# Storing both split parts of a weight tile and reading them back by GpSimd transfers, in an attention and two-expert-layer kernel

## The chip, the core and the metric

The kernel runs on one core of a Trainium2 chip. The metric is the device time of one execution in microseconds (us), the median over several runs. A profile is the record of one execution; its rows name the engines PE (TensorE matmul), PEld (TensorE weight load), DVE (VectorE), ACT (ScalarE), POOL (GpSimd) and SP (SyncE, which here only issues transfers).

## What is computed

Attention over 4 batches, 12 heads, 448 tokens and head size 64 with normed queries and keys, then two feed-forward layers on the 1792 tokens of 768 features:

```python
q_n, k_n = rmsnorm(q, g_q), rmsnorm(k, g_k)
attn = softmax(q_n @ k_n.T / sqrt(64))
x = attn @ v                                  # (4*448, 768)
h = x @ w_in                                  # 768 -> 2048
x = where(h > 0, h, exp(min(h, 0)) - 1) @ w_out          # 2048 -> 768
xn = x / rms(x) * rms_g
x = (silu(xn @ w_gate) * (xn @ w_val)) @ w_out2          # 768 -> 1536 -> 768
```

Everything is float32 in DRAM, and the result is wanted to about that precision.

## The kernel before

**Products.** A float32 product is made of three products of split operands: each operand is cut into a high part, rounded to the type that TensorE multiplies at one pass (F32R), and a low part, the rest (`split_w`, `split_x`, `split_g`). `mm3` multiplies high by high, high by low and low by high into one bank of PSUM. Data lie transposed, features on partitions, 448 tokens of one batch in a row; one matmul is 128x128 by 128x448.

**Stages.** `STAGES` has five. Stage 0 is the first layer for batch 0, stage 1 the same for batch 1, stage 2 the second layer for batches 0 and 1, stage 3 the first layer for batches 2 and 3, stage 4 the second layer for batches 2 and 3. The attention of batch 0 fills the first 75 us or so; that of the later batches is woven into stages 0 to 2. Where two batches stand together (from the second group of stage 2 on, `PLAIN`), four blocks of weights and four of data are multiplied as a "quad" of seven block products instead of eight (`quad`, `take_duo`), which wants sums and differences of weight blocks.

**Weights.** `wst` is a stream of chunks of 6 blocks of 128x128, 64 bits a weight. `w_convert` loads a raw chunk (768 KB, ring `wr` of two tiles), and ACT or POOL and DVE make it a float32 chunk (ring `wc`, three tiles). `w_f32` stores that chunk to DRAM (`kept`, 384 KB) at its first use, and later uses load it from there. `split_w` then makes the split tile (ring `w`, four tiles of two parts, 768 KB each; from stage 3 on two more, shown as `late`): a copy that rounds (ACT, DVE or POOL), and a subtraction (DVE or POOL). For a quad, `w_split` first makes sums and differences of two chunks in `p` tiles (four subtractions of half chunks), then splits four tiles, of which the fourth is half as wide. So each use of a weight costs a load, a copy and a subtraction, and that of a quad's weights the sums besides. `w_ahead` keeps as many tiles split ahead of the matmuls as the ring has.

**Between the stages.** Before a second layer, `norm` sums squares on TensorE, takes a root on ACT and a reciprocal on DVE (448 columns, one for each batch). The data of the next stage's quads are combined and split too (`combo`).

**Order.** All instructions are collected as operations with prices (`plan.add`). `Plan.schedule` lays them out by a list scheduler with a random seed and a number of passes, picks the engine where an operation has several (`alts`), and issues them in that order. Each engine then works its list in order. All transfers but a few small ones stand in SP's list, so a transfer whose data aren't ready holds back those behind it. Line numbers in the profile are those of a helper (L331, L334 in the changed kernel); operations are told apart by tiles.

Of the kernel before, what the change touches and what calls it, by code (L numbers as in the profile page):

```python
# [10 lines left out]
F32 = mybir.dt.float32  # L11
# [9 lines left out]
P = 128  # L21
# [15 lines left out]
class Plan:  # L37
# [4 lines left out]
    PASSES = 22  # L42
    SEED = 17
# [131 lines left out]
    def forward(self, rank):  # L175
# [35 lines left out]
        while left:  # L211
# [95 lines left out]
def kernel(ctx: ExitStack, tc: tile.TileContext, dims, tok, qk, vr, gq, gk, wst, rmsg, ident_in, out):  # L307
# [114 lines left out]
    def transposes(pairs):  # L422
        def go():
            for o, i in pairs:
                T.transpose(o, i, ident)

        plan.add({"pe": (0.02 + 0.11 * len(pairs), go)}, [o for o, _ in pairs], [i for _, i in pairs] + [ident], lag=0.16)
# [159 lines left out]
    def steps_of(kind, plain):  # L587
        nums = list(one if kind == 1 else two)
        res, k = [], 0
        nf = NF1 if kind == 1 else 2 * NF2  # L590
        for g in range(len(nums) // (nf + OG)):
            if g < plain:
                res += [("c", n) for n in nums[k:k + nf + OG]]
                k += nf + OG
# [8 lines left out]
            k += nf + OG  # L603
        return res

    stream = [st for s, (kind, _) in enumerate(STAGES) for st in steps_of(kind, PLAIN[s])]
# [7 lines left out]
    uses = {}  # L614
    for kind, _ in STAGES:
        for n in one if kind == 1 else two:
            uses[n] = uses.get(n, 0) + 1

    def w_f32(n):
# [5 lines left out]
        if uses[n] > 1:  # L625
# [13 lines left out]
    def w_split():  # L639
# [7 lines left out]
        if j == 0:  # L647
# [6 lines left out]
            duo["c"] = (c0, sa, sb, c1[:, HW:WN])  # L654
        spl_w[i] = split_w(duo["c"][j], HW if j == 3 else WN)

# [167 lines left out]
    def s_group(i, *gs):  # L824
# [17 lines left out]
        block(mms, (0.0 if gs == (0,) else 0.3) + 0.62 * len(gs))  # L842
# [82 lines left out]
    def pv(i, kts):  # L925
# [13 lines left out]
        block(mms, 0.14 + 0.866 * len(kts))  # L939
# [82 lines left out]
    def mm3(o, w, x, first, last):  # L1022
        wh, wl = w
        xh, xl = x
        block([(o, wh, xh, first, False), (o, wh, xl, False, False), (o, wl, xh, False, last)], 0.612)
# [282 lines left out]
    def second_experts(bs, plain):  # L1308
# [6 lines left out]
        for f0 in range(0, CF2, NF2):  # L1315
            last = f0 + NF2 >= CF2
# [12 lines left out]
            yield from acc_units(bs, f0, NF2, f0 == 0, last, ob, True, o_done)  # L1329
# [37 lines left out]
    for s, (kind, bs) in enumerate(STAGES):  # L1367
# [9 lines left out]
        for step in first_experts(bs, s >= 3) if kind == 1 else second_experts(bs, PLAIN[s]):  # L1377
# [105 lines left out]
```

## Time and profile before

| | us |
|---|---|
| median of 3 runs | 1238.09 (1236.55 to 1240.48) |
| the profiled execution | 1236.46 |
| its span | 1234.7 |
| TensorE busy, of the span | 1201.6 (97%) |
| DVE, POOL, ACT busy | 883.5, 903.7, 720.9 |
| moved by DMA | 178.95 MB, 145 GB/s in the mean |

TensorE is the busiest engine by far, and 33.1 us of the span are left in which it does not multiply. The weights are at work in these stretches: stage 0 from about 95 to 277 us, stage 1 to 435, stage 2 to 735, stage 3 to 980, stage 4 to the end. POOL spends the largest share of its time on weights: 226.8 us on 120 subtractions `w<-wc,w`, 64.5 on 32 of `w<-p,w` and 45.4 on 48 copies `w<-wc`; ACT spends 77.8 us on 99 such copies. A busy share says little by itself here: the question in each stretch is whether TensorE waits, and for whom.

### The profile page before, as it was taken

What the parts mean: (1) busy time and instruction counts of PE and PEld (TensorE: products, weight loads), DVE (VectorE), ACT (ScalarE), POOL (GpSimd) and SP (SyncE); (2) the same over time, 40 slices, a digit from 0 to 9 for tenths busy, and PEclk for the clock granted to TensorE, in tenths of its full rate; (3) what the DMA queues carried; (4) which work ended last, traced back from release to release, by engine and by line L of the source; (5) the groups of instructions that cost most, each with busy time, mean ns of one, the idle gap of its engine ahead of it and who ended that gap; (6) DMA issues with size and microseconds to landing.
All of it is one profiled execution on the core that took longest, in us unless ns stands there. A gap on an engine that the chain in (4) does not pass through costs nothing.

```text
span 1234.7 us, 17825 instructions
## 1 busy us (share of the span) xinstructions
PE 1201.6 (97%) x6228; PEld 1009.7 (82%) x6228; DVE 883.5 (72%) x1332; ACT 720.9 (58%) x1413; POOL 903.7 (73%) x651
## 2 busy tenths in 40 slices
PE   3999999999999999999999999999999989999998
PEld 2557877778777787777999999999999979999998
DVE  6887988878544578645797899825435899397592
ACT  5996879768665678655564563643425843342240
POOL 3467888789655586746998899967566998698590
PEclk9999999999999999999999999999999999999999
DMA  7578788775444366644336545212112112112112
GB/s 258 183 234 257 264 291 271 259 229 162 152 138 128 125 202 229 197 140 159 128 129 222 177 168 191 77 53 77 53 52 64 40 51 65 51 65 77 40 52 90
DMA packets 65664, 178.95 MB, mean 145 GB/s; under 512 B 11039, under 2 KB 23333, under 8 KB 65573
## 3 DMA queue, kind: packets, MB, share of 16 engines
q1 hardware_dynamic: 56932, 168.82, 41.0%
q10 hardware_dynamic: 8640, 8.99, 2.5%
q8 instruction: 49, 0.80, 0.3%
q14 instruction: 43, 0.34, 0.1%
HBM read 139.86 MB, written 37.92 MB: 144 GB/s over the span
## 4 chain that ended last, share of the span: by engine, by line
PE 88%; DVE 5%; ACT 2%; DMA 2%; issue 1%; POOL 1%; SPq 0%; ACTq 0%; DVEq 0%
PE bank L331 88%; DVE tbig L331 2%; DMA wr<-wst 1%; DVE rw L331 1%; ACT tbig L331 1%; DVE w L331 1%; DMA ybig<-tok 0%; DMA rb<-scr 0%; ACT p L331 0%; DVE bank L331 0%; POOL w L331 0%; DVE ybig L331 0%; DVE ss L331 0%; DVE ql L331 0%; DMA wc<-kept 0%
## 5 line engine op out<-in xcount | busy, mean ns | idle before, releaser
L331 PE MATMUL bank<-gbig,w 128*128 128x448 f32 x1872 | 402.7, 369 | 1.4 <-DVE tbig L331 1.0
L331 PEld LDWEIGHTS bank<-gbig,w 128*128 128x128 f32 x1872 | 346.4, 188 | 37.6 <-issue 7.1
L331 PE MATMUL bank<-xs,w 128*128 128x448 f32 x1584 | 364.5, 371 | 1.8 <-DVE tbig L331 1.1
L331 PEld LDWEIGHTS bank<-xs,w 128*128 128x128 f32 x1584 | 290.6, 188 | 31.9 <-issue 7.1
L331 POOL TENSOR_TENSOR w<-wc,w 128x768 fp32r<-128x768 f32 (+1 forms) x120 | 226.8, 1892 | 54.4 <-ACT w L331 48.2
L331 DVE TENSOR_REDUCE bank<-bank 128x1 f32<-128x448 f32 x168 | 98.9, 624 | 42.8 <-PE bank L331 42.5
L331 ACT ACTIVATE w<-wc 128x768 fp32r<-128x768 f32 (+1 forms) x99 | 77.8, 786 | 74.0 <-PE bank L331 60.5
L331 ACT ACTIVATE p<-bank,nm,rr 128x448 f32<-128x448 f32 x126 | 90.3, 720 | 22.6 <-DVE nm L331 16.3
L331 DVE SCALAR_TENSOR_TENSOR wc<-wc,wt 128x768 int32<-128x768 int32 x68 | 88.3, 1298 | 21.0 <-ACT wc L331 12.4
L331 PE MATMUL bank<-late,w 128*128 128x448 f32 x420 | 100.6, 366 | 0.8 <-DVE w L331 0.8
L331 ACT ACTIVATE pt<-bank 128x384 f32<-128x384 f32 (+2 forms) x175 | 75.7, 451 | 22.9 <-PE bank L331 20.6
L331 POOL TENSOR_TENSOR gbig<-tbig,gbig 128x448 fp32r<-128x448 f32 x57 | 76.9, 1354 | 13.5 <-ACT gbig L331 12.8
L331 PEld LDWEIGHTS bank<-late,w 128*128 128x128 f32 x420 | 78.8, 188 | 7.7 <-DVE w L331 1.2
L331 POOL TENSOR_TENSOR w<-p,w 128x768 fp32r<-128x768 f32 x32 | 64.5, 2017 | 20.2 <-ACT w L331 19.7
L331 POOL TENSOR_SCALAR w<-wc 128x768 fp32r<-128x768 f32 (+1 forms) x48 | 45.4, 947 | 44.4 <-PE bank L331 35.1
L331 DVE TENSOR_TENSOR ybig<-bank,ybig 128x448 f32<-128x448 f32 x72 | 44.3, 620 | 44.2 <-PE bank L331 43.7
L331 PE MATMUL bank<-ident,p 128*128 128x128 f32 x441 | 70.8, 279 | 1.2 <-ACT pe L331 0.8
L331 ACT ACTIVATE wt<-wr 128x768 uint16<-128x768 uint8 x51 | 55.7, 1093 | 24.8 <-DVE wc L331 20.1
L331 PEld LDWEIGHTS bank<-ident,p 128*128 128x128 f32 x441 | 53.7, 142 | 19.0 <-ACT pt L331 3.3
L331 PE MATMUL bank<-xs,late 128*128 128x448 f32 x288 | 68.2, 366 | 0.9 <-DVE xs L331 0.6
L331 DVE TENSOR_SCALAR wt<-wr 128x768 uint16<-128x768 uint16 x68 | 68.5, 1008 | 0.3
L331 ACT ACTIVATE tbig<-bank 128x448 f32<-128x448 f32 x78 | 42.1, 541 | 39.8 <-PE bank L331 31.9
(237 smaller groups left out, 2229.2 us busy)
## 6 DMA issues: line engine op xcount, KB each, us to landing
wr<-wst SPq DMA_DIRECT2D x68, 768.0 KB
wc<-kept SPq DMA_DIRECT2D x100, 384.0 KB
kept<-wc SPq DMA_DIRECT2D x68, 384.0 KB
rw<-qk SPq DMA_DIRECT2D x21, 512.0 KB
tk<-tok SPq DMA_DIRECT2D x20, 480.0 KB
rv<-vr SPq DMA_DIRECT2D x24, 256.0 KB
out_t<-ybig SPq DMA_DIRECT2D x24, 224.0 KB
rb<-scr ACTq DMA_DIRECT2D x36, 128.0 KB
```

Source lines behind the costliest of these rows:

```text
L331: return lambda *a, **k: f(*[real(x) for x in a], **{n: real(x) for n, x in k.items()})
```

## The change

`store_parts` writes a split tile, both parts, to DRAM at its first use (768 KB, the half-wide tile 2 x 192 KB), unless the tile isn't used again. `load_parts` brings it back at each later use, by a transfer that GpSimd issues, so that copy, subtraction and sums fall away there. The float32 chunk is kept only where it is used both plainly and in a quad. Stage 4 takes its three groups of weights in the order 1, 2, 0 (`TURN`), where groups 1 and 2 were quads in stage 2 already, and group 0, which was plain there, still has its sums to be made. The scheduler gets other prices for a few TensorE blocks, 14 passes instead of 22 and seed 3 instead of 17, and so lays out everything anew.

In instructions of the program, before and after: `kept` stores 68 and 24, `kept` loads 100 and 24, stores of parts 0 and 92 (76 of 768 KB, 16 of 192 KB), GpSimd loads 0 and 136 (96 of 768 KB, 40 of 192 KB); on POOL, weight subtractions 176 and 89, weight copies 56 and 28, sums of `p` 86 and 54; on ACT, weight copies 167 and 80; on DVE, weight subtractions 48 and 19. The matmuls are the same in number and shape.

```diff
-    PASSES = 22
-    SEED = 17
+    PASSES = 14
+    SEED = 3
...
             if self.ops[i][4]:
-                if e == "sp":
+                if e == "g":
+                    dma_free = max(free[e], dma_free) + self.ops[i][2]
+                    done[i] = dma_free + self.DMA_LAT
+                elif e == "sp":
...
-        q, cost = (SP, 0.43) if by == "sp" else (A, 0.5)
+        q, cost = {"sp": (SP, 0.43), "a": (A, 0.5), "g": (G, 1.0)}[by]
...
+    TURN = {4: (1, 2, 0)}
...
+    def load_parts(k):
+        w = r_w.next()
+        if k[1] == 3:
+            for h in range(2):
+                dma(w[:, h, 0:HW], parts[k][:, h * HW:(h + 1) * HW], P * HW * 4, by="g")
+        else:
+            dma(w.rearrange("p a n -> p (a n)"), parts[k], P * WN * 8, by="g")
+        return w
...
+        parts[k] = tc.dram_tile([P, 2 * WN], F32, name=f"parts{len(parts)}")
+        dma(parts[k], w.rearrange("p a n -> p (a n)").bitcast(F32), P * WN * 8)
...
         c = w_convert(n)
-        if uses[n] > 1:
+        if n in plain_uses and n in in_quads:
...
         if st[0] == "c":
+            k = (st[1], 0)
+            if k in parts:
+                spl_w[i] = load_parts(k)
+                return
             spl_w[i] = split_w(w_f32(st[1]), WN)
+            if plain_uses[st[1]] > 1 or st[1] in in_quads:
+                store_parts(k, spl_w[i])
             return
...
+        if k in parts:
+            spl_w[i] = load_parts(k)
+            return
...
         spl_w[i] = split_w(duo["c"][j], HW if j == 3 else WN)
+        if quad_uses[n0, n1] > 1:
+            store_parts(k, spl_w[i])
...
-        for f0 in range(0, CF2, NF2):
-            last = f0 + NF2 >= CF2
+        for f0 in [NF2 * g for g in turn]:
+            last = f0 == NF2 * turn[-1]
```

The first rows of SP's list, before: `tok` and `qk` are inputs of the attention, `tk`, `wr`, `ybig` and `rw` tiles that hold them (the raw weight tiles `wr` serve for this at the start).

```order
L331 DMA tk_101<-tok 128x960
L331 DMA rsb_127<-gq 1x128
L331 DMA wr_91<-tok 128x960
L331 DMA rw_102<-qk 128x1024
L331 DMA rsb_127<-gk 1x128
L331 DMA ident<-ident_in 128x128
L331 DMA ybig<-tok 128x960
L331 DMA wr_92<-qk 128x1024
L331 DMA ybig<-tok 128x960
```

After:

```order
L334 DMA tk_101<-tok 128x960
L334 DMA wr_91<-tok 128x960
L334 DMA rsb_127<-gk 1x128
L334 DMA rsb_127<-gq 1x128
L334 DMA ident<-ident_in 128x128
L334 DMA ybig<-tok 128x960
L334 DMA rw_102<-qk 128x1024
L334 DMA wr_92<-qk 128x1024
L334 DMA ybig<-tok 128x960
```

The first load into `ybig` (`tok`, 480 KB) has moved ahead of the first load of `rw` (`qk`, 512 KB).

SP's list in the middle of stage 0, before: a raw weight load (`wr<-wst`, 768 KB) alternates with the store of a float32 chunk (`kept<-wc`, 384 KB).

```order
L331 DMA wr_92<-wst 128x1536
L331 DMA kept_157<-wc_94 128x768
L331 DMA wr_91<-wst 128x1536
L331 DMA tk_101<-tok 128x960
L331 DMA kept_158<-wc_95 128x768
L331 DMA wr_92<-wst 128x1536
L331 DMA kept_159<-wc_93 128x768
L331 DMA wr_91<-wst 128x1536
L331 DMA tk_101<-tok 128x960
L331 DMA kept_162<-wc_94 128x768
L331 DMA rw_102<-qk 128x1024
```

After:

```order
L334 DMA wr_91<-wst 128x1536
L334 DMA parts_155<-w_97 128x1536
L334 DMA parts_157<-w_98 128x1536
L334 DMA wr_92<-wst 128x1536
L334 DMA rw_102<-qk 128x1024
L334 DMA parts_159<-w_99 128x1536
L334 DMA wr_91<-wst 128x1536
L334 DMA tk_101<-tok 128x960
L334 DMA kept_162<-wc_95 128x768
L334 DMA parts_161<-w_100 128x1536
L334 DMA wr_92<-wst 128x1536
L334 DMA parts_163<-w_97 128x1536
```

The stores in between are now `parts<-w` of 768 KB, which wait for a finished split tile, and a raw load stands behind one or two of them.

DVE's list at the change from stage 3 to stage 4, before, up to the first of the two reciprocals of `norm`: three instructions make weight tiles of the next quads (`w_100<-p`, `w_99<-wc`, `p_107<-wc,wc`).

```order
L331 TENSOR_TENSOR bank_131<-bank_131,rsb_126 128x448
L331 TENSOR_TENSOR w_100<-p_106,w_100 128x768
L331 TENSOR_TENSOR tbig<-bank_130,rsb_126 128x448
L331 TENSOR_TENSOR gbig<-tbig,gbig 128x448
L331 TENSOR_TENSOR tbig<-bank_133,tbig 128x448
L331 TENSOR_TENSOR w_99<-wc_95,w_99 128x768
L331 TENSOR_TENSOR tbig<-tbig,ybig 128x448
L331 TENSOR_TENSOR xs_73<-ybig,xs_72 128x448
L331 TENSOR_TENSOR p_107<-wc_95,wc_93 128x384
L331 TENSOR_TENSOR tbig<-bank_132,tbig 128x448
L331 RECIPROCAL tbig<-tbig 128x448
```

After:

```order
L334 TENSOR_TENSOR tbig<-bank_130,rsb_126 128x448
L334 TENSOR_TENSOR xs_67<-ybig,xs_66 128x448
L334 TENSOR_TENSOR gbig<-tbig,gbig 128x448
L334 TENSOR_TENSOR tbig<-bank_133,tbig 128x448
L334 TENSOR_TENSOR late_5489<-ybig,late_5464 128x448
L334 TENSOR_TENSOR tbig<-bank_132,tbig 128x448
L334 TENSOR_TENSOR xs_73<-ybig,xs_72 128x448
L334 TENSOR_TENSOR bank_131<-bank_131,rsb_126 128x448
L334 TENSOR_TENSOR tbig<-bank_133,tbig 128x448
L334 TENSOR_TENSOR xs_87<-ybig,xs_86 128x448
L334 RECIPROCAL tbig<-tbig 128x448
```

No weight instruction stands there now; the rest is the attention's and the norm's, with two more subtractions of split data (`late`, `xs_87`) moved up.

## Rows read from the trace of the kernel before

**Rows 1.** The page: busy time of each engine; one group of weight subtractions.

```profile
PE 1201.6 (97%) x6228; PEld 1009.7 (82%) x6228; DVE 883.5 (72%) x1332; ACT 720.9 (58%) x1413; POOL 903.7 (73%) x651
...
L331 POOL TENSOR_TENSOR w<-wc,w 128x768 fp32r<-128x768 f32 (+1 forms) x120 | 226.8, 1892 | 54.4 <-ACT w L331 48.2
```

**Rows 2.** Busy time of each engine by stretch; the first line names the columns.

```profile
core 0: us, PE busy (x) PEld busy (x) DVE busy (x) ACT busy (x) POOL busy (x), PEclk, DMA share, GB/s
0.00:75.00 75.00, 53.26 (x302) 30.93 (x303) 56.60 (x147) 59.26 (x141) 28.83 (x30) 0.95 0.65 216
75.00:150.00 75.00, 73.20 (x404) 55.17 (x404) 63.55 (x99) 58.92 (x123) 57.20 (x43) 1.00 0.79 259
...
300.00:425.00 125.00, 123.40 (x693) 93.59 (x693) 69.57 (x143) 77.87 (x189) 73.45 (x58) 1.00 0.44 140
...
735.00:975.00 240.00, 240.00 (x1180) 221.29 (x1179) 146.50 (x185) 116.53 (x204) 183.12 (x131) 1.00 0.25 82
975.00:1025.00 50.00, 45.57 (x215) 39.34 (x214) 49.55 (x51) 28.25 (x47) 48.31 (x36) 1.00 0.10 32
1025.00:1225.00 200.00, 200.00 (x988) 185.31 (x988) 141.43 (x182) 65.24 (x105) 146.62 (x101) 1.00 0.20 62
1225.00:1234.70 9.70, 6.13 (x31) 5.34 (x29) 2.50 (x4) 0.00 (x0) 0.00 (x0) 1.00 0.28 109
```

**Rows 3.** Waits of TensorE from 975 to 1025: us in total, times, longest.

```profile
PE bank L331 <- DVE w L331: 1.6, 2, 0.8
PE bank L331 <- DVE tbig L331: 1.1, 2, 0.7
PE bank L331 <- DVE ql L331: 0.8, 1, 0.8
PE bank L331 <- DVE xs L331: 0.6, 1, 0.6
PE bank L331 <- DVE xf L331: 0.3, 1, 0.3
```

**Rows 4.** Groups on DVE, 983 to 1020: count, busy us, mean ns, idle before.

```profile
L331 DVE RECIPROCAL tbig<-tbig 128x448 f32<-128x448 f32 x2 | 5.9, 2939 | 0.0
L331 DVE TENSOR_TENSOR w<-p,w 128x768 fp32r<-128x768 f32 x3 | 5.1, 1690 | 0.0
...
L331 DVE TENSOR_TENSOR w<-wc,w 128x768 fp32r<-128x768 f32 (+1 forms) x2 | 2.5, 1231 | 0.0
...
L331 DVE TENSOR_TENSOR p<-wc,wc 128x384 f32<-128x384 f32 x1 | 1.5, 1507 | 0.0
```

**Rows 5.** Groups on POOL, the same stretch.

```profile
L331 POOL TENSOR_TENSOR late<-wc,late 128x384 fp32r<-128x384 f32 (+1 forms) x2 | 2.9, 1431 | 0.0
...
L331 POOL TENSOR_TENSOR p<-wc,wc 128x384 f32<-128x384 f32 x1 | 1.0, 1016 | 0.0
```

**Rows 6.** SP's transfers in order of time: start us, us, queue, transfer.

```profile
64.38 0.34 SPq L331 DMA_DIRECT2D wr<-wst  x1
...
248.33 0.39 SPq L331 DMA_DIRECT2D wr<-wst  x1
```

**Rows 7.** Stretches with much transfer; the columns are those of Rows 2.

```profile
65.00:250.00 185.00, 183.09 (x1008) 136.56 (x1007) 155.66 (x257) 151.58 (x320) 144.16 (x102) 1.00 0.78 265
120.00:125.00 5.00, 5.00 (x30) 4.04 (x29) 4.90 (x9) 4.34 (x11) 2.75 (x3) 1.00 0.99 307
...
230.00:240.00 10.00, 10.00 (x56) 8.90 (x57) 7.78 (x15) 8.02 (x17) 7.43 (x7) 1.00 0.98 370
```

**Rows 8.** The chain of waits in order of time: start us, us, what.

```profile
3.12 6.15 DMA ybig<-tok
...
28.06 7.18 DMA wr<-wst
...
395.85 3.06 DMA wc<-kept
```

**Rows 9.** Instructions on the raw tile: ns min/median/max, first and last start.

```profile
L331 DVE TENSOR_SCALAR wt<-wr x68: 596/850/2292, 27.3 to 735.6; 128x768 uint16<-128x768 uint16 x68
```

More of the change, by code (lines that the diff above doesn't have):

```diff
@@ L425, in go @@
                 T.transpose(o, i, ident)
-        plan.add({"pe": (0.02 + 0.11 * len(pairs), go)}, [o for o, _ in pairs], [i for _, i in pairs] + [ident], lag=0.16)
+        plan.add({"pe": (0.109 * len(pairs) - 0.055 * (len(pairs) > 1), go)}, [o for o, _ in pairs], [i for _, i in pairs] + [ident], lag=0.16)
     def copy(dst, src, eng="vag"):
@@ L585, with steps_of @@
     OG = NF1 * CD // CW
-    def steps_of(kind, plain):
+    TURN = {4: (1, 2, 0)}
+    def steps_of(kind, plain, s):
         nums = list(one if kind == 1 else two)
-        res, k = [], 0
+        res = []
         nf = NF1 if kind == 1 else 2 * NF2
-        for g in range(len(nums) // (nf + OG)):
+        for g in TURN.get(s, range(len(nums) // (nf + OG))):
+            k = g * (nf + OG)
             if g < plain:
                 res += [("c", n) for n in nums[k:k + nf + OG]]
-                k += nf + OG
                 continue
@@ L602, in steps_of @@
             res += [("c", nums[k + nf + j]) for j in range(OG)]
-            k += nf + OG
         return res
-    stream = [st for s, (kind, _) in enumerate(STAGES) for st in steps_of(kind, PLAIN[s])]
+    stream = [st for s, (kind, _) in enumerate(STAGES) for st in steps_of(kind, PLAIN[s], s)]
     spl_w = {}
@@ L609, with store_parts @@
     kept = {}
[L614 to L617, printed above, removed]
+    plain_uses, quad_uses = {}, {}
+    for st in stream:
+        if st[0] == "c":
+            plain_uses[st[1]] = plain_uses.get(st[1], 0) + 1
+        elif st[1] == 0:
+            quad_uses[st[2:]] = quad_uses.get(st[2:], 0) + 1
+    in_quads = {n for p in quad_uses for n in p}
+    parts = {}
+    def load_parts(k):
[6 more added lines that the diff above has]
+        return w
+    def store_parts(k, w):
+        if k[1] == 3:
+            parts[k] = tc.dram_tile([P, WN], F32, name=f"parts{len(parts)}")
+            for h in range(2):
+                dma(parts[k][:, h * HW:(h + 1) * HW], w[:, h, 0:HW].bitcast(F32), P * HW * 4)
+            return
+        parts[k] = tc.dram_tile([P, 2 * WN], F32, name=f"parts{len(parts)}")
+        dma(parts[k], w.rearrange("p a n -> p (a n)").bitcast(F32), P * WN * 8)
     def w_f32(n):
@@ L643, in w_split @@
         if st[0] == "c":
+            k = (st[1], 0)
+            if k in parts:
+                spl_w[i] = load_parts(k)
+                return
             spl_w[i] = split_w(w_f32(st[1]), WN)
+            if plain_uses[st[1]] > 1 or st[1] in in_quads:
+                store_parts(k, spl_w[i])
             return
         _, j, n0, n1 = st
-        if j == 0:
+        k = ((n0, n1), j) if 0 < j < 3 else ((n0, 0) if j == 0 else (n1, 3))
+        if j == 0 and ((n0, n1), 1) not in parts:
             c0, c1 = w_f32(n0), w_f32(n1)
@@ L654, in w_split @@
             duo["c"] = (c0, sa, sb, c1[:, HW:WN])
+        if k in parts:
+            spl_w[i] = load_parts(k)
+            return
+        if j == 3 and (n1, 0) in parts:
+            w = spl_w[i] = r_w.next()
+            for h in range(2):
+                dma(w[:, h, 0:HW], parts[n1, 0][:, h * WN + HW:(h + 1) * WN], P * HW * 4, by="g")
+            return
         spl_w[i] = split_w(duo["c"][j], HW if j == 3 else WN)
+        if quad_uses[n0, n1] > 1:
+            store_parts(k, spl_w[i])
     def w_convert(n):
@@ L938, in pv @@
                     mms.append((o[a], v[a, 4 * h + 3], pe[a, 64 * h:64 * h + S], False, True))
[L939 removed]
+        block(mms, 0.3 + 0.7515 * len(kts))
         if 3 not in kts:
@@ L1024, in mm3 @@
         xh, xl = x
-        block([(o, wh, xh, first, False), (o, wh, xl, False, False), (o, wl, xh, False, last)], 0.612)
+        block([(o, wh, xh, first, False), (o, wh, xl, False, False), (o, wl, xh, False, last)], 0.608)
     gs = {}
@@ L1306, in gv_unit, with second_experts @@
         yield
-    def second_experts(bs, plain):
+    def second_experts(bs, plain, turn):
         ob = {}
@@ L1328, in second_experts @@
                 widen(bs)
-            yield from acc_units(bs, f0, NF2, f0 == 0, last, ob, True, o_done)
+            yield from acc_units(bs, f0, NF2, f0 == NF2 * turn[0], last, ob, True, o_done)
             if f0 + NF2 == plain * NF2:
@@ L1376 @@
                     norm(b)
-        for step in first_experts(bs, s >= 3) if kind == 1 else second_experts(bs, PLAIN[s]):
+        for step in first_experts(bs, s >= 3) if kind == 1 else second_experts(bs, PLAIN[s], TURN.get(s, range(CF2 // NF2))):
             if step == "late":
```

2 lines of the change are left out of this document (1 added, 1 removed).

## The prediction

> **What bounds the kernel now.** I read the page's first part, then the table of busy time by stretch, then TensorE's waits where it is short of full, and last the groups, transfers and chain of those places. TensorE multiplies for 1201.6 of 1234.7 us [rows 1], and the change leaves its matmuls alone, so at most 33.1 us can be won. The table by stretch says where they lie [rows 2]: 75.00 - 53.26 = 21.7 us before 75, 1.8 from 75 to 150, 1.6 from 300 to 425, 50.00 - 45.57 = 4.4 from 975 to 1025, and 9.70 - 6.13 = 3.6 in the tail. Elsewhere TensorE is full: from 735 to 975 it shows 240.00 of 240 us, 1180 matmuls, 0.203 us each, at a granted clock of 1.00. Most of the weight work that the change takes away lies in such full stretches, where DVE, ACT and POOL have idle time and TensorE waits for none of them. It is worth nothing there. The question is what happens in the few places that aren't full, and whether the new transfers spoil a full one.
>
> **The boundary of stages 3 and 4 (975 to 1025).** Here alone DVE (49.55 of 50.00) and POOL (48.31) are both full [rows 2], and every one of TensorE's listed waits names DVE: w 1.6, tbig 1.1, ql 0.8, xs 0.6, xf 0.3, together 4.4 us [rows 3]. DVE makes weights for the first quads of stage 4 there: three subtractions w<-p (5.1 us), two w<-wc (2.5) and one sum p<-wc,wc (1.5), 9.1 us, among them two reciprocals of 2.94 us that the norm needs [rows 4]. POOL has seven rows of such groups between 983 and 1020, ten instructions, 13.8 us, of which the first and the last stand in [rows 5]. After the change DVE's list holds no weight instruction there, and POOL's only transfers: stage 4 begins with group 1, whose parts lie in DRAM, and six tiles of the ring can be loaded ahead. DVE would fall to some 40 of 50 us and POOL to some 35 plus a few issues. The 1.6 us for w go. The other 2.8 us are attention, data and norm that stood behind weights, and most go too; the two reciprocals stay, and some tenths with them. I take -3.6, with ends 0 (the room is refilled by data work) and -4.4 (all).
>
> **Stage 0.** Here transfers grow. Between the 3rd and the 33rd raw weight tile (64 to 248 us [rows 6]) SP's list had 30 stores of float32 chunks (384 KB). Now it has 29 stores of both parts (768 KB, 22.8 MB) and 15 of chunks, so 15 x 0.393 = 5.9 MB fewer of these: +16.9 MB. From 65 to 250 the core moved 265 GB/s, 49.0 MB in 185 us, with the DMA engines at a share of 0.78 [rows 7]. With 65.9 MB it is 356 GB/s. What the engines can move is read from three rows: 265 / 0.78 = 340 by the mean, 307 in a stretch with a share of 0.99, 370 in another with 0.98 [rows 7]. So the same bytes take 194, 215 or 178 us against 185: +9, +30 or nothing. The load isn't even, and the raw loads can run ahead by two tiles only; but a lead of a few us can also be lost without TensorE waiting, and stage 0 was bounded by TensorE (183.09 of 185 busy [rows 7]). I take +0.8, from the 370 of the row with most bytes, since what is added are large packets like those there; ends 0 and +9. The +30 would need the whole stretch to move as the 5 us of mixed small loads did, and I leave it out.
>
> The stretch of 10 us moved 370 GB/s. [...]
>
> **The start.** The first load into ybig is on the chain with 6.15 us [rows 8], and is now issued ahead of a 512 KB load. At the 370 GB/s of the fullest stretch [rows 7] 512 KB take 1.4 us. That is the most it can gain; but the displaced load (rw) feeds the first scores, so it can cost as much on that side: +1 to -1.4. I take -0.7.
>
> **The small waits.** 1.8 us from 75 to 150 and 1.6 from 300 to 425 [rows 2]. In the latter the chain has a load of a kept chunk, 3.06 us [rows 8], ahead of copy and subtraction; with parts only a load is left. I take -0.5, ends 0 and -3.4.
>
> **The full stretches.** Of 176 weight subtractions on POOL 89 are left. The page's group of 120 such costs 226.8 us, 1892 ns each [rows 1], and half of them is 113 us. POOL gets 136 issues of transfers. No row of before shows a GpSimd transfer, so one issue is bounded by SP's 0.34 us [rows 6] and by the shortest weight instruction on POOL at the boundary, 1.0 us [rows 5]: 46 to 136 us, spread over the 950 us from stage 1 on. Against it stand also 28 copies and 32 sums taken away, so POOL doesn't become busier on the whole. In the full stretches this nets to zero, since POOL is idle for 57 of 240 us there [rows 2].
>
> **The tail.** Stage 4 ends with group 0 now, in the same form (last products, one addition, one store): 0. From 1025 to 1225 TensorE is full at 200.00 [rows 2] with all weight work done there; two thirds of it become loads, so 0.
>
> **The sum:** -3.6 - 0.7 + 0.8 - 0.5 + 0 = -4.0. The profiled execution took 1236.46 us with a span of 1234.7, so it becomes 1232.5; the median of the runs is 1.6 higher, and against it the sum gives **1234.1**, which I round to 1234.0. About 0.3%, 3.7 us, is what a measurement of this kernel can tell from no change: below 1234.4 is faster, above 1241.8 slower.
>
> **Rivals.** *The gain doesn't show at the boundary.* Only the 1.6 us for w go, and the norm is next late: 5.9 us of reciprocals stand on one engine between the last addition of stage 3 and the first use of the scale, and the combining of data, moved up into the room, meets POOL's. With the start at 0 and stage 0 at +0.8 this is -0.8 to -1.6, **1237**: no change. For it speaks that four of the five waits at the boundary aren't for w [rows 3]; against it that DVE gets 9 us of room.
>
> *The stores of stage 0 fill the DMA engines* (the other side). A raw load stands on SP's queue behind one or two stores of parts; these wait for a split tile, which waits for TensorE to free a slot of the ring. From 356 GB/s on, the load of the next raw tile comes late, then its conversion, and TensorE waits for w. With 340 GB/s it costs +9 us, against -4.8 from the rest: **1242 to 1243**, slower; half of it is 1238, no change. For it: the mean of a share of 0.78 leaves 22% room and the bytes grow by 34%. Against it: 370 GB/s was moved for 10 us, and stores are not urgent.
>
> *The GpSimd loads land late.* POOL works in order, so a load that waits for its ring slot holds back POOL's subtractions of data, and the other way round. A load of 768 KB landed after 7.18 us beside other transfers [rows 8]; a quad is 63 matmuls, 63 x 0.203 = 12.8 us. It decides when landings exceed 12.8 us: at 15 us, 2.2 us on each of the 8 quads of groups 1 and 2 in stage 4 is +18, **1252**. For it: nobody has shown such a transfer here; against it: the stretch moves 62 GB/s at a share of 0.20 [rows 2].
>
> A DVE instruction on the raw tile took 2.29 us at most, the last at 735.6 us [rows 9]. [...]
>
> That the change doesn't do what it says is out: the loads and stores stand in the lists of POOL and SP.
>
> **How the numbers follow.** Forecast 0.45 (faster, 1229 to 1234); gain not shown 0.25 (same); stage 0 saturated 0.20, of which 0.04 is partial and the same, 0.16 slower; GpSimd late 0.10, slower. So faster 0.45, same 0.29, slower 0.26. The low end is the sum of the lower bounds, -4.4 - 1.4 - 3.4 = -9.2, so 1229; the high end takes in most of the saturated case, +9 with no gain elsewhere, 1246 to 1247; what lies above belongs mostly to late loads. Range **1229 to 1246**.
>
> **What would show it.** Right: idle time of TensorE from 975 to 1025 at 1 us or less, with no w or p rows on DVE; waits for w absent between 100 and 280 although the DMA rate there is near 350 GB/s; the first load into ybig landed before 9.3 us (3.12 + 6.15 [rows 8]). Wrong: TensorE waits for w behind DMA wr<-wst in stage 0; waits of TensorE on transfers of parts in stages 1 to 4; or tbig, xs and the reciprocals still named at the boundary with the old size.

## The result, and the profile after

The changed kernel takes 1246.56 us (median of 5, 1242.65 to 1248.66) against 1238.40 before: a ratio of 1.0068, 95% interval 1.0055 to 1.0081. It is 8.2 us slower, where 4 us faster was forecast, and lies just above the range. Half of the weight subtractions on POOL fell away as planned, and the place that the prediction looked at, the boundary of stages 3 and 4, did gain what it said. The time went elsewhere.

The profiled execution is the fastest of the five (1242.65 us, span 1240.9). Its page, to be read beside [rows 1]: TensorE's busy time, the group of GpSimd loads (count, busy us, mean ns), and the issues of the loads with their median us to landing.

```profile
PE 1207.1 (97%) x6228; PEld 1011.1 (81%) x6228; DVE 820.8 (66%) x1313; ACT 655.4 (53%) x1308; POOL 733.4 (59%) x647
...
L334 POOL DMA_DIRECT2D w<-parts x103 | 57.9, 563 | 139.0 <-PE bank L334 130.0
...
w<-parts POOLq DMA_DIRECT2D x79, 768.0 KB, 5.1
...
late<-parts POOLq DMA_DIRECT2D x17, 768.0 KB, 6.1
```

TensorE's busy time is 5.5 us more for the same matmuls, so not all of the loss is waiting. The table by stretch, with the columns of [rows 2]:

```profile
core 0: us, PE busy (x) PEld busy (x) DVE busy (x) ACT busy (x) POOL busy (x), PEclk, DMA share, GB/s
0.00:75.00 75.00, 54.12 (x295) 32.16 (x297) 53.40 (x143) 56.97 (x138) 32.63 (x33) 0.91 0.64 214
75.00:150.00 75.00, 74.36 (x411) 56.02 (x408) 63.20 (x96) 59.93 (x122) 55.87 (x43) 1.00 0.95 354
150.00:300.00 150.00, 143.86 (x778) 108.72 (x777) 123.24 (x200) 110.15 (x226) 107.62 (x84) 1.00 0.96 345
300.00:425.00 125.00, 125.00 (x705) 96.23 (x705) 61.14 (x145) 76.52 (x190) 53.35 (x61) 1.00 0.65 210
735.00:975.00 240.00, 239.67 (x1174) 219.96 (x1173) 136.04 (x188) 96.22 (x170) 140.69 (x134) 1.00 0.53 176
975.00:1025.00 50.00, 48.28 (x234) 43.37 (x233) 46.24 (x54) 25.72 (x45) 34.69 (x36) 1.00 0.44 146
1025.00:1225.00 200.00, 199.71 (x981) 183.84 (x980) 109.10 (x162) 42.13 (x73) 93.80 (x102) 1.00 0.46 145
1225.00:1240.90 15.90, 12.25 (x61) 11.02 (x59) 3.73 (x6) 0.00 (x0) 0.00 (x0) 0.95 0.25 97
```

Against [rows 2] the boundary (975 to 1025) idles 1.72 us where it idled 4.43, and 300 to 425 doesn't idle at all where it idled 1.60. But 150 to 300, which was full, now idles 6.14 us, and there and from 75 to 150 the DMA engines have a share of 0.96 and 0.95 (before: 0.73 and 0.79). At the start the granted clock is lower: 0.91 on the mean against 0.95. The row of before from 150 to 300, which [rows 2] leaves out:

```profile
150.00:300.00 150.00, 150.00 (x818) 116.08 (x817) 123.24 (x204) 120.23 (x250) 124.80 (x87) 1.00 0.73 247
```

TensorE's longest waits from 150 to 300 (us in total, times, longest) name the attention, not the weights:

```profile
PE bank L334 <- POOL ql L334: 3.3, 2, 2.2
PE bank L334 <- ACT pt L334: 1.3, 2, 0.9
PE bank L334 <- DVE rs L334: 1.2, 2, 0.7
```

And the chain there names transfers (start, us, what). A raw weight tile and a 4 KB transfer of the attention stand in it for 9 to 11 us each.

```profile
224.65 8.77 DMA wr<-wst
...
267.65 10.74 DMA scr<-rr
```

At the boundary, to be read beside [rows 3], no wait for w is left, and of the DVE groups of [rows 4] only the two reciprocals are:

```profile
PE bank L334 <- DVE ybig L334: 0.9, 1, 0.9
PE bank L334 <- DVE late L334: 0.8, 1, 0.8
```

Busy shares hide part of this, because the profile's busy time counts slow matmuls as work. One more reading of all traces helps: how much later (us, + is later) than in the kernel before the same amount of matmul work had been started, each matmul counted by its columns. Cut at the times of the trace of before, it says where each kernel loses or gains. One execution each; the second execution of the changed kernel ("again") shows how far that carries.

| | 0 to 75 | 75 to 300 | 300 to 425 | 425 to 975 | 975 to 1025 | 1025 on | sum |
|---|---|---|---|---|---|---|---|
| changed | +1.3 | +6.8 | -2.3 | +2.9 | -3.9 | +1.4 | +6.1 |
| again | +1.5 | +11.5 | -2.3 | +2.5 | -3.9 | +0.8 | +10.1 |
| small_stores | +3.0 | +2.7 | -2.4 | +2.3 | -3.9 | +0.9 | +2.6 |
| fat_stores | +2.4 | +10.1 | +0.1 | 0.0 | -0.1 | 0.0 | +12.5 |
| plan_only2 | -1.1 | +4.9 | +0.7 | +1.4 | +0.3 | +1.4 | +7.6 |
| seed_18 | -0.8 | +6.5 | +0.4 | +3.5 | -2.6 | +0.3 | +7.3 |
| old_plan | -3.7 | +12.8 | +0.5 | +2.4 | -2.7 | +2.0 | +11.2 |
| parts_18 | +1.9 | +19.5 | -2.0 | +1.9 | -5.2 | +0.4 | +16.5 |
| second_only | -2.4 | +9.3 | -1.1 | +10.9 | -0.6 | +0.5 | +16.6 |
| first_only | +1.4 | +10.5 | -1.1 | +3.5 | -2.1 | +0.4 | +12.6 |
| second_use | -1.4 | +14.5 | 0.0 | +3.2 | -5.9 | +0.1 | +10.6 |
| no_turn | -0.1 | +9.8 | -1.6 | +0.8 | -2.0 | 0.0 | +6.8 |
| held_second | -0.7 | -0.6 | +0.2 | +2.2 | -2.8 | +1.5 | -0.2 |
| held_second_18 | +1.6 | 0.0 | +0.3 | +2.6 | -5.5 | 0.0 | -1.0 |
| held_before | +2.2 | -0.4 | +0.1 | +1.9 | -1.4 | +0.6 | +3.0 |

### The profile page after: what moved, and what is told of

It is laid out like the page before. It is cut to its first block, busy times and chain, and to the rows that moved or that the text cites. A ratio compares the mean times of both kernels' runs of the same rounds, so it can differ in the third digit from the quotient of the medians.

```text
span 1240.9 us, 17697 instructions
## 1 busy us (share of the span) xinstructions
PE 1207.1 (97%) x6228; PEld 1011.1 (81%) x6228; DVE 820.8 (66%) x1313; ACT 655.4 (53%) x1308; POOL 733.4 (59%) x647
## 4 chain that ended last, share of the span: by engine, by line
PE 81%; DVE 7%; DMA 6%; ACT 3%; issue 1%; POOL 1%; ACTq 0%; SPq 0%; DVEq 0%; POOLq 0%
PE bank L334 81%; DVE wc L334 1%; DMA wr<-wst 1%; DMA scr<-rr 1%; DVE tbig L334 1%; DVE bank L334 1%; DMA rw<-qk 1%; DVE wt L334 1%; DMA tk<-tok 1%; DMA rsb<-rsum 1%; POOL ql L334 1%; DMA ybig<-tok 1%; DVE ybig L334 1%; ACT p L334 1%; ACT tbig L334 0%
## 5 line engine op out<-in xcount | busy, mean ns | idle before, releaser
L334 PE MATMUL bank<-gbig,w 128*128 128x448 f32 x1872 | 407.9, 370 | 1.0 <-ACT ybig L334 0.4
L334 POOL DMA_DIRECT2D w<-parts x103 | 57.9, 563 | 139.0 <-PE bank L334 130.0
L334 POOL TENSOR_TENSOR w<-wc,w 128x768 fp32r<-128x768 f32 (+1 forms) x56 | 107.2, 1915 | 22.4 <-ACT w L334 15.8
L334 DVE SCALAR_TENSOR_TENSOR wc<-wc,wt 128x768 int32<-128x768 int32 x68 | 91.3, 1342 | 18.4 <-ACT wc L334 10.4
L334 POOL TENSOR_TENSOR gbig<-tbig,gbig 128x448 fp32r<-128x448 f32 x51 | 65.8, 1295 | 25.0 <-ACT gbig L334 24.2
L334 POOL TENSOR_TENSOR w<-p,w 128x768 fp32r<-128x768 f32 x25 | 48.8, 1953 | 50.2 <-ACT w L334 49.9
L334 DVE TENSOR_SCALAR wt<-wr 128x768 uint16<-128x768 uint16 x68 | 72.4, 1064 | 5.7 <-DMA wr<-wst 5.7
L334 ACT ACTIVATE wt<-wr 128x768 uint16<-128x768 uint8 x54 | 58.8, 1089 | 29.5 <-DMA wr<-wst 13.3
L334 ACT ACTIVATE w<-p 128x768 fp32r<-128x768 f32 x28 | 23.6, 843 | 94.2 <-PE bank L334 84.5
L334 DVE TENSOR_TENSOR tbig<-bank,tbig 128x448 f32<-128x448 f32 x77 | 46.7, 617 | 35.8 <-ACT tbig L334 27.0
```

Source lines behind the costliest of these rows:

```text
L334: return lambda *a, **k: f(*[real(x) for x in a], **{n: real(x) for n, x in k.items()})
```

## Experiments, first round: is it the stores of stage 0, or the layout?

**again.** The changed kernel as it is.

> The changed kernel unaltered, for a second profiled execution. Accounting so far (changed against before, one execution each, time at which the same amount of matmul work had been done): start +1.4 us by 75, stage 0 (75 to 300) +6.7, 300 to 480 -2.4, 480 to 970 +2.9 without a wait, boundary of stages 3 and 4 -3.8, stage 4 +1.3. If these are the change's, they come back within some 2 us each and the ratio is 1.006 to 1.008. If the +2.9 of 480 to 970 (matmuls spaced 206.7 ns instead of 202.7 for long stretches) is chance of one execution, it moves by more than half.

Ratio 1.0053 (1.0036 to 1.0071), a little below what was expected. The gains come back to a tenth (-2.3, -3.9), and the loss from 425 to 975 comes back too (+2.5 after +2.9), so it isn't chance. The loss of stage 0 grows to +11.5, by more than the 2 us expected: it is the part that varies.

**plan_only, plan_only2.** The kernel before with the changed kernel's numbers for the scheduler, and no parts.

```diff
-    PASSES = 22
-    SEED = 17
+    PASSES = 14
+    SEED = 3
...
-    plan.add({"pe": (0.02 + 0.11 * len(pairs), go)}, ...)
+    plan.add({"pe": (0.109 * len(pairs) - 0.055 * (len(pairs) > 1), go)}, ...)
```

(and the three other TensorE prices of the change.)

> The kernel before with the new seed, passes and TensorE prices alone. Theory (transfers): the loss is from the stores of stage 0, so this one stays within 0.3% of before, 1235 to 1242, with TensorE full from 150 to 300. Rival (order): the new layout by itself costs the start (the longer stretch at the lower clock, +1.4) and some of the rest: 1241 to 1247, with idle time of TensorE in stage 0.

1.0069 (1.0044 to 1.0094): the rival's value, though not a byte more is moved. The same kernel was run again:

> The kernel before with the new seed, passes and TensorE prices again, for a profile at the full clock. Its first timing was 1.0069 (1.0044 to 1.0094) against before, which the transfers cannot explain. Theory (order): 1.004 to 1.009 again, and the profile shows the loss as waits in 75 to 300, as in the changed kernel, though with the DMA share of before (0.7 to 0.8). Rival (pace and start): no waits there, but a longer stretch at the lower clock and longer stretches of matmuls spaced 206.7 ns.

1.0056 (1.0037 to 1.0076). The loss is spread: +4.9 in 75 to 300, in small waits with the DMA share of before, and +3.8 from 300 on.

**seed_18.** The kernel before with one number changed.

```diff
-    SEED = 17
+    SEED = 18
```

> The kernel before with nothing changed but the scheduler's seed, 17 to 18. If the layout of before is one of many equal ones: 0.998 to 1.002. If it is a lucky one, so that any new layout costs: 1.003 to 1.010, and then the changed kernel's loss against before is to be put first to the new layout.

1.0075 (1.0056 to 1.0094). So the layout of before is a good draw: two others of the same work, with no part stored, cost 0.6 to 0.8%. The row of 75 to 300 for both (plan_only2 first), in the columns of the table above:

```profile
75.00:300.00 225.00, 220.61 (x1193) 167.44 (x1192) 186.93 (x295) 177.10 (x360) 166.64 (x122) 1.00 0.74 247
```

```profile
75.00:300.00 225.00, 219.12 (x1185) 164.93 (x1182) 189.72 (x293) 172.77 (x357) 171.93 (x123) 1.00 0.74 249
```

TensorE idles 4.4 and 5.9 us in 225 with the transfers of before (0.74, 247 and 249 GB/s). A comparison of two kernels whose schedules were laid anew is thus a comparison of two draws; only pairs with the same order tell what bytes cost.

**old_plan.** The change with seed, passes and prices of before.

```diff
-    PASSES = 14
-    SEED = 3
+    PASSES = 22
+    SEED = 17
```

> The change with the seed, the passes and the TensorE prices of before: parts stored and read back, group order 1, 2, 0, another layout. Theory (the new plan's numbers cost, the parts gain): it drops below the changed kernel and below before, ratio 0.994 to 0.999. Rival (transfers of stage 0 cost, whatever the layout): 1.003 to 1.008 with 5 us and more idle between 75 and 300.

1.0073 (1.0055 to 1.0091), with +12.8 in 75 to 300, where TensorE idles 8.8 us. The theory (the new numbers cost, the parts gain) fell, and the number is the rival's. But this run doesn't show the rival's cause either: with parts the operations are others, and seed 17 lays stage 0 otherwise than before, so that bytes and layout are mixed.

**second_only, first_only.** Parts for one layer only; the other keeps float32 chunks.

```diff
     def store_parts(k, w):
+        if (k[0][0] if isinstance(k[0], tuple) else k[0]) < N1:
+            return
...
-        if n in plain_uses and n in in_quads:
+        if n < N1 or n in plain_uses and n in in_quads:
```

(with `>= N1` for first_only.)

> The changed kernel with parts stored and read back for the second layer alone; the first layer keeps float32 chunks as before. Theory (stores of stage 0): stage 0 is full again (0 to 1 us idle from 150 to 300) and the boundary stays at 1 to 2 us idle, so the ratio against before is 0.995 to 1.000. Rival (order, or GpSimd transfers as such): stays at 1.003 to 1.008.

> The changed kernel with parts for the first layer alone; the second layer keeps float32 chunks. Theory (stores of stage 0): it has the loss of stage 0 (4 to 7 us idle from 150 to 300) and not the gain of the boundary (4 us idle from 975 to 1025), so the slowest of the four, 1.008 to 1.012. Rival (order, or GpSimd transfers of the second layer): close to before, 0.998 to 1.003.

second_only 1.0066 (1.0033 to 1.0098), first_only 1.0098 (1.0060 to 1.0136). first_only lies where the theory had it. second_only has the rival's number: without a new byte in stage 0 (243 GB/s from 75 to 300) it loses +9.3 there, and in its execution the granted clock fell to 0.5 four times for 3.4 us after the start (at 116.5, 488.6, 751.4 and 1010.8 us). As both are new layouts, neither tells the two causes apart.

## Experiments, second round: the same order, other bytes

**small_stores.** The changed kernel's order on every engine, with fewer bytes in the stores of stage 0. The kernel leaves out most of each such tile, and its later loads bring as many bytes of another input.

```diff
-            dma(w.rearrange("p a n -> p (a n)"), parts[k], P * WN * 8, by="g")
+            src, at = (any_data, small_at[k]) if k in small_at else (parts[k], None)
+            dma(w.rearrange("p a n -> p (a n)"), src, P * WN * 8, by="g", after=at)
...
+        if k[1] == 0 and k[0] < N1:
+            dma(parts[k].rearrange("p (a n) -> p a n", a=2)[:, :, 0:96], w[:, :, 0:96].bitcast(F32), P * WN * 8)
+            small_at[k] = len(plan.ops) - 1
+            return
         dma(parts[k], w.rearrange("p a n -> p (a n)").bitcast(F32), P * WN * 8)
```

> The changed kernel, every engine's list in the same order, but the stores of parts of the first layer move 1/8 of their bytes (both parts, 96 of 768 columns each); their later loads read as many bytes of another input, so the products of those weights are not the reference's. Theory (bytes of stage 0 fill the DMA engines): the loss between 150 and 300 (+7.6 and +11.0 us in two executions) falls to under 2, and the ratio to 0.997 to 1.001. Rival (the order: raw loads stand behind stores that wait for a split tile): the loss stays at 5 us or more.

1.0011 (0.9999 to 1.0023). The loss of 75 to 300 falls from +6.8 and +11.5 to +2.7, a little above the 2 us of the theory, and all else behind it stays (-2.4, +2.3, -3.9, +0.9). So the change without these bytes takes as long as the kernel before, within the noise: its gains of 6.3 us pay for its new layout, and no more.

**fat_stores.** The mirror: the order of before on every engine, with the stores of float32 chunks of stage 0 made two or three times as large.

```diff
-            kept[n] = tc.dram_tile([P, WN], F32, name=f"kept{n}")
-            dma(kept[n], c, P * WN * 4)
+            m = 2 + n % 2 if n < N1 else 1
+            fat = tc.dram_tile([P, m, WN], F32, name=f"kept{n}")
+            kept[n] = fat[:, 0]
+            dma(fat, c.rearrange("p (o n) -> p o n", o=1).to_broadcast([P, m, WN]) if m > 1 else c.rearrange("p (o n) -> p o n", o=1), P * WN * 4)
```

> The kernel before, every engine's list in the same order, but each store of a float32 chunk of the first layer writes the chunk two or three times in turn (384 KB become 768 or 1152), so that stage 0 moves some 17 MB more, as in the changed kernel, with no other wait. Theory (bytes): 4 to 8 us lost between 75 and 300, DMA share there 0.93 and over, ratio 1.004 to 1.007. Rival (the stores' waits or the layout, not bytes): under 2 us lost, ratio below 1.002.

1.0079 (1.0062 to 1.0096), the way the theory said and above its range. The profiled execution loses +10.1 in 75 to 300, and 0.1 or less in every stretch after that; it is the clearest row of the study. Some 1.5 us of the 10.1 (an estimate, see the last section) come of 3.4 us at half the granted clock, from 148.3 on. Before, changed, small_stores and fat_stores from 75 to 300:

```profile
75.00:300.00 225.00, 223.20 (x1220) 171.25 (x1221) 186.79 (x302) 179.15 (x371) 182.00 (x129) 1.00 0.75 251
```

```profile
75.00:300.00 225.00, 218.22 (x1187) 164.74 (x1184) 186.44 (x295) 170.08 (x347) 163.49 (x127) 1.00 0.95 348
```

```profile
75.00:300.00 225.00, 221.49 (x1208) 168.48 (x1204) 191.24 (x303) 173.54 (x355) 167.55 (x130) 1.00 0.79 258
```

```profile
75.00:300.00 225.00, 217.08 (x1167) 162.20 (x1166) 174.41 (x289) 168.66 (x351) 168.05 (x123) 0.99 0.92 330
```

The mechanism is in the waits of the engines that convert raw weights, in the same stretch (those of 1.5 us and over; us in total, times, longest). Before:

```profile
ACT wc L331 <- DMA wr<-wst: 4.5, 3, 2.7
POOL wc L331 <- DMA wr<-wst: 4.8, 3, 2.5
```

Changed:

```profile
ACT wt L334 <- DMA wr<-wst: 5.9, 5, 1.9
ACT wc L334 <- DMA wr<-wst: 1.7, 3, 0.7
DVE wt L334 <- DMA wr<-wst: 5.7, 3, 2.4
POOL wc L334 <- DMA wr<-wst: 9.8, 7, 4.0
```

small_stores, and then fat_stores:

```profile
ACT pt L334 <- DMA wr<-wst: 2.7, 1, 2.7
DVE wt L334 <- DMA wr<-wst: 1.6, 1, 1.6
POOL wc L334 <- DMA wr<-wst: 4.6, 2, 3.2
```

```profile
ACT wc L331 <- DMA wr<-wst: 14.9, 10, 3.7
ACT wt L331 <- DMA wr<-wst: 1.6, 2, 1.1
POOL wc L331 <- DMA wr<-wst: 10.3, 4, 6.4
```

In these rows the engines wait for raw tiles (`wr<-wst`) 9.3 us before, 23.1 in the changed kernel, 8.9 with small stores, 26.8 with fat ones. Raw loads stand behind stores on SP's queue, and with the DMA engines at a share of 0.92 to 0.95 they land later: where the landing of a raw tile set an engine free, it came 6.2 us after the issue in the median before, 7.5 in the changed kernel (6.9 in its second execution), 5.6 with small stores and 7.1 with fat ones. That slow stores hold their own tiles too long is not seen: ACT, DVE and POOL wait 0.8 us for a store in the changed kernel, and not at all with fat stores.

How a late raw tile reaches TensorE can be followed once in the changed kernel, in the lists of POOL and of TensorE (start, us, instruction, idle time before it). POOL waits 4.04 us for a raw tile, and the subtractions of the attention (`ql`) behind it in its list are what TensorE then waits 2.18 us for:

```profile
233.57 1.31 POOL L334 TENSOR_SCALAR wc<-wr 128x768 f32<-128x768 f32 x1 [4.04 <-DMA wr<-wst]
...
236.24 4.01 POOL L334 TENSOR_TENSOR ql<-rw,qh 128x512 fp32r<-128x512 f32 x2
```

```profile
240.30 0.47 PE L334 MATMUL bank<-qh,ql 128*128 128x448 f32 x1 [2.18 <-POOL ql L334]
```

For TensorE's other waits this path is likely, but not shown. And the waits for raw tiles alone don't give the loss: the second execution of the changed kernel has 21.1 us of them and loses more (+11.5), and seed_18, another layout, has 8.0 and loses +6.5.

The price of stage 0's bytes, in one order, is 1.0053 to 1.0068 less 1.0011, some 5 to 7 us, and 9.8 us in the order of before. Each pair has the same lists, and differs in the bytes of its stores (small_stores also in what its later loads bring).

**second_use.** Tiles of the first layer stored in stage 1 instead.

```diff
     def store_parts(k, w):
+        if (k[0][0] if isinstance(k[0], tuple) else k[0]) < N1 and wpos["spl"] <= N1:
+            return
```

> The change, but tiles of the first layer are stored in stage 1 (where the core moved 140 GB/s) instead of stage 0, which stores float32 chunks as before; stage 1 splits again, stages 3 and 4 read parts back. Theory (bytes of stage 0 plus a toll of any new layout): stage 0 near the 2 to 6 us that new layouts without parts lost from 75 to 300, the boundary kept (-3 to -4): ratio 1.000 to 1.005. Rival (bytes cost wherever they go): 1.006 to 1.010.

1.0077 (1.0062 to 1.0092): the rival's number, but not by its cause, as the loss is +14.5 in 75 to 300, where little was added (257 GB/s against 251), and nothing in stage 1. It is one more layout that costs, and 6.8 us at half the granted clock, from 117.5 on, are part of it.

**parts_18.** The change with seed 18 and the prices of before.

> The change with seed 18 and the passes and prices of before, to stand beside the kernel before with seed 18 (1.0075). Three layouts without parts gave 1.000 (seed 17), 1.0056 and 1.0069 (two timings of one), 1.0075; two with parts 1.0053 to 1.0068 and 1.0073. If the parts are worth nothing over layouts (gains of about 6 us at 300 to 425 and the boundary, bytes of stage 0 about -6): 1.004 to 1.009. If they gain and seed 18 is bad by itself: 1.000 to 1.004.

1.0135 (1.0120 to 1.0150), above both ranges: +19.5 in 75 to 300. Whether the 13 us over seed_18's +6.5 are the bytes' or one more layout's, this run doesn't tell, as seed 18 lays other operations here.

**no_turn.** The group order of before.

```diff
-    TURN = {4: (1, 2, 0)}
+    TURN = {}
```

> The change without the order 1, 2, 0: stage 4 begins with group 0, whose sums and splits are made anew. Theory (the boundary's gain is the missing weight work on DVE): TensorE is idle 4 to 5 us from 975 to 1025 as before, where the changed kernel had 1.7, and DVE shows subtractions into w there; ratio 1.007 to 1.010. Rival (the gain is the layout's): 1 to 2.5 us idle there all the same.

1.0066 (1.0050 to 1.0083). The boundary idles 3.36 us (row of 975 to 1025), and DVE has weight work there again (a sum and a subtraction), less than in [rows 4]:

```profile
975.00:1025.00 50.00, 46.64 (x225) 41.45 (x224) 46.39 (x53) 31.82 (x52) 41.77 (x36) 1.00 0.27 80
```

```profile
L334 DVE TENSOR_TENSOR p<-wc,p 128x384 f32<-128x384 f32 x1 | 1.5, 1500 | 0.8 <-POOL w L334 0.8
L334 DVE TENSOR_TENSOR w<-p,w 128x768 fp32r<-128x768 f32 x1 | 1.4, 1377 | 0.0
```

That lies between theory (4 to 5) and rival (1 to 2.5): half of the gain is lost with the order (-2.0 against -3.9). The comparison is a close one, as all engines' lists are the changed kernel's up to 922 us. For the same reason its +9.8 from 75 to 300 is a third execution of the changed order there, between +6.8 and +11.5. In the whole time the order can't be seen: 1.0066 against 1.0053 to 1.0068.

## Experiments, third round: the layout of the first 300 us held

The scheduler orders operations by ranks. I took the ranks that it had found for the kernel before, for the 2419 operations that the two programs have in common at their beginning (start, stages 0 and 1), and held them; the rest is laid anew. In the traces all engines' lists are those of before up to 447 us.

```diff
         for _ in range(self.PASSES + 1):
+            rank[:len(HELD)] = HELD
             got = self.forward(rank)
```

**held_second, held_second_18, held_before.** Parts for the second layer alone, as in second_only, with seed 17 and 18; and no parts with seed 18.

> Parts for the second layer alone (group order 1, 2, 0, prices of before), with the ranks by which the scheduler of before ordered its operations held for all operations up to stage 1, so that start, stage 0 and stage 1 are laid out as before; the scheduler lays the rest anew. Theory (the loss is the bytes and the new layout of the first 300 us; the parts gain 2 to 4 us at the boundary): nothing lost before 425, -2 to -4 at the boundary, ratio 0.996 to 1.000, below both kernels. Rival (parts or a new layout cost also later, by waits or by the slower spacing of matmuls): 1.001 to 1.005 with the loss after 425.

> The same with seed 18 for what is laid anew, to see how much the layout of the later part alone moves the time. Theory: within 0.2% of the same kernel with seed 17, 0.996 to 1.001. Rival (any layout but the one of before costs, also late): the two differ by over 0.3%, or both lie above 1.002.

> No parts: the kernel before with its own ranks held up to stage 1 and seed 18 for the rest, the control for the two others and for the kernel before with seed 18 throughout (1.0075). Theory (the toll of a new layout falls in the first 300 us): 0.999 to 1.003, the boundary idle 2 to 4 us. Rival (the toll is spread over the kernel): 1.004 and more.

0.9996 (0.9986 to 1.0006), 0.9971 (0.9960 to 0.9981) and 1.0009 (0.9998 to 1.0020). From 75 to 300 the three lie at -0.6, 0.0 and -0.4: the toll is gone. held_before against seed_18 (1.0009, 1.0075) is the same seed with and without the held part: the toll of that layout falls almost wholly there. With the same seed, parts against no parts give 0.9971 / 1.0009 = 0.9962, 4.7 us, of which 0.4 us lie outside the core's span (2.2 us of held_before, 1.8 of the other). The table shows 5.5 - 1.4 = 4.1 at the boundary; some 1.5 of these (an estimate) are 3.4 us at half the granted clock, which the profiled execution of held_before has from 997.0 on and the other hasn't. held_second_18 is faster than both kernels, 1234.08 us against 1237.85. Its rows for 75 to 300, 425 to 975 and the boundary, where TensorE idles 0.82 us:

```profile
75.00:300.00 225.00, 223.04 (x1220) 170.79 (x1217) 184.03 (x302) 178.87 (x373) 182.54 (x130) 1.00 0.76 252
425.00:975.00 550.00, 547.82 (x2776) 481.00 (x2777) 393.56 (x522) 304.60 (x549) 407.62 (x290) 1.00 0.55 188
975.00:1025.00 50.00, 49.18 (x242) 45.03 (x241) 46.92 (x58) 25.35 (x45) 40.07 (x40) 1.00 0.49 158
```

The two seeds differ by 0.25%, more than the 0.2% that I expected: held_second gains -2.8 at the boundary instead of -5.5, where its granted clock is at 0.5 for 3.4 us from 995.5, and loses 1.5 from 1025 on. Its 0.9996 can't be told from the kernel before.

## Why the prediction was wrong, step by step

The forecast sum was -4.0, and the first row of the table has +6.1. Of these 10 us 6 lie from 75 to 300, where +0.8 was taken; in the second execution 10.7 of 14. That the time came out at the upper end of the range is luck: the end was worked out as +9 in stage 0 with no gain elsewhere, while the runs have both gains (-2.3 and -3.9) and more loss than that.

**The boundary: right, the close agreement in part by luck.** -3.6 was forecast and -3.9 measured, twice. The waits for w and the weight groups on DVE are gone. But TensorE still idles 1.72 us, not 1 or less, and DVE fell to 46.24 us, not 40, all of it data and norm work now. What is the parts' own is less certain than the agreement looks: layouts without parts show +0.3, -2.6 and -1.4 there, those with second-layer parts and the turned order -3.9, -2.7, -5.2, -5.9, -2.8, -5.5 and -0.6. The means are -1.2 and -3.8, so some 2.6 us belong to the parts and the order together. Part of the scatter is the clock: plan_only2, held_before, old_plan, second_only and held_second have 3.4 us at half clock in this stretch, and the others none.

**The small waits: right in sign, too small.** -0.5 was taken within 0 to -3.4; 300 to 425 alone gave -2.3. Where stage 1 reads parts the table shows -1.1 to -2.4, but for old_plan (+0.5); where it doesn't, +0.7, +0.4 and 0.0 (plan_only2, seed_18, second_use), but for second_only (-1.1).

**Stage 0: the term that failed.** +0.8 was taken, between 0 and +9, without a sum that gives it (178 us for 185 gives nothing); the bytes cost 5 to 7 us in the changed order and 9.8 in that of before. The step "I take +0.8, from the 370 of the row with most bytes" compared totals: 356 GB/s wanted, 370 possible, so it fits. The changed kernel did move 348 GB/s at a share of 0.95, which gives 366 at a share of one, an estimate; the rate was read well, and the conclusion was wrong. With the engines not yet full (fat_stores, share 0.92, 330 GB/s) the raw loads already came late (26.8 us of waits for them on ACT and POOL), and the lead of two raw tiles didn't hide it. The rival "the stores of stage 0 fill the DMA engines" had the place and the first steps (raw tile late, conversion late), and nearly the time (1242 to 1243); it should have been the likeliest. Its last step was another: it let TensorE wait for w, and TensorE waited for the attention's work (ql 3.3, pt 1.3 and rs 1.2 us from 150 to 300), which in the one case that was followed stood behind a conversion. So the sign of being right, no waits for w at a rate near 350 GB/s, was met while stage 0 lost 7 to 11 us: it looked at the wrong wait. The point from which the rival decides, 356 GB/s, was put too high. Nor was the 370 of the row with most bytes a ceiling: from 125 to 150 the changed kernel moved 413 GB/s, at a share of 1.02.

**The term that wasn't there: the layout.** The prediction saw that the scheduler "lays out everything anew" and priced only the two places in which the order had visibly moved. A new order by itself cost 0.6 to 0.8% in two draws (plan_only, seed_18), mostly in waits of the first 300 us that no single edit causes. That the kernel before sat in a good draw could be suspected from its trace: 150 to 300, with all four engines above 75% busy, idled 0.00 us.

**The start: no verdict.** -0.7 was forecast; +1.3 and +1.5 came, with TensorE at half clock for 13.65 us from 27.5, against 6.83 before. But held_before has the start's order of before and shows the same 13.65 us and +2.2, held_second 6.83 us and -0.7. And fat_stores, with the same order and no half clock there, shows +2.4. It varies with the execution by some 3 us, more than the term, and what moves it stays open. The sign that was named did come: the first load into ybig was used at 7.36 us instead of 9.29. But the second such load then stood in the chain, used at 11.52 instead of 11.71, and TensorE's first long piece of work began at 14.94 instead of 15.15: a gain of 0.2 us.

**425 to 975: not foreseen.** +2.9 and +2.5, of which waits are the smaller part (TensorE idles 0.46 us there in the profiled execution of the changed kernel); see the last section.

**GpSimd loads late: rightly ruled unlikely.** The median landing is 5.1 and 6.1 us against the 12.8 that it needed, one wait of 0.3 us names a load, and an issue costs POOL 563 ns, within the bounds of 0.34 to 1.0. The longest landing was 9.9 us.

## What to carry to other kernels

Ask of a queue that feeds an in-order pipeline how late each transfer lands, not whether the sum of bytes fits: at a DMA share of 0.92 (fat_stores) and 0.95 (the changed kernel) the engines already waited 26.8 and 23.1 us for raw tiles, and once, in the changed kernel, a TensorE wait of 2.18 us could be followed back to such a tile. When a change makes a scheduler lay out everything anew, the new layout is an edit of its own with a price (here 0.6 to 0.8% in two draws, as large as the change), to be measured with one seed changed and nothing else. And hold the order fixed when an effect is to be isolated: altering only the bytes of existing transfers, or holding the ranks of a part, gave the three clean answers of this study.

## What the runs showed of the hardware

In these traces TensorE has two paces for the same chain of 448-column matmuls at a granted clock of 1.00. Rows of the changed kernel from 582 to 622 and 845 to 882, of its second execution at the same places of the program, and of before:

```profile
582.00:622.00 40.00, 40.00 (x199) 37.05 (x199) 22.67 (x24) 23.42 (x36) 34.61 (x25) 1.00 0.66 226
845.00:882.00 37.00, 37.00 (x181) 33.60 (x180) 14.20 (x24) 8.71 (x16) 16.55 (x17) 1.00 0.46 157
```

```profile
586.00:626.00 40.00, 40.00 (x200) 36.78 (x197) 22.95 (x24) 23.14 (x35) 33.94 (x26) 1.00 0.64 222
850.00:886.00 36.00, 36.00 (x176) 32.70 (x175) 13.70 (x23) 8.55 (x15) 16.06 (x17) 1.00 0.47 159
```

```profile
582.00:622.00 40.00, 40.00 (x199) 37.06 (x198) 26.42 (x26) 22.59 (x37) 36.94 (x26) 1.00 0.35 110
845.00:882.00 37.00, 37.00 (x185) 34.28 (x184) 16.22 (x22) 8.88 (x15) 19.66 (x14) 1.00 0.15 43
```

In the first stretch all show 199 or 200 in 40 us (one per 202.7 ns in the trace, apart from one gap). In the second the changed kernel shows 181 in 37 us and 176 in 36, before 185 in 37: one per 206.7 ns against 202.7, in an unbroken run. The slower pace begins and ends without a wait, at the same matmuls in both executions of one program, and takes other places in another. It doesn't follow the bytes: the first stretch moved 226 GB/s at the faster pace, the second 157 at the slower; and fat_stores keeps the pace of before (the same row of 735 to 975, 1180 matmuls, as in [rows 2]):

```profile
735.00:975.00 240.00, 240.00 (x1180) 221.42 (x1179) 146.53 (x188) 114.50 (x199) 183.69 (x129) 1.00 0.29 89
```

Nor is it the order of the instructions alone: no_turn, whose lists are the changed kernel's up to 922 us, has the faster pace from 845 to 882.

```profile
845.00:882.00 37.00, 37.00 (x185) 34.32 (x184) 15.59 (x25) 10.09 (x18) 18.04 (x19) 1.00 0.47 160
```

From 425 to 975 the changed kernel has some 800 matmuls at the slower pace, and the kernel before some 340. At 4 ns each that is 1.8 us of the +2.9 there, an estimate. What sets the pace stays open.

The granted clock fell from 1.0 to 0.5 for 3.4 us, or once 6.8, in the midst of nine of the table's executions: second_only four times, parts_18 three, old_plan twice, and once each in fat_stores (148.3 us), first_only (225.9), second_use (117.5), plan_only2, held_before and held_second (995 to 998). There the matmuls start 373 ns apart instead of 203 (0.37 us also at the half clock of the changed kernel's start, from 28.15 to 28.52 us), so 3.4 us cost some 1.5 (an estimate from the two spacings). Shortly before each fall TensorE had stood for 1.1 to 2.7 us in one piece, in second_use for 3.3 us across it. But it also stood for 2.1 to 3.3 us in one piece without a fall after it: in the changed kernel at 238 us, in its second execution twice, in first_only at 112, in old_plan at 483, and in parts_18 at 194 and 300. What brings a fall about isn't shown. The kernel before shows a half clock only from 30.1 to 36.9 us, the changed kernel only from 27.5 to 41.2 and in its last 1.6 us.
